# Sums and the gate-times-up product moved to GpSimd, and the runs of a seven-product scheme dealt to other gaps

## The chip, the cores and the metric

The kernel runs on one core of one Trainium2 chip. The metric is the device time of one execution in microseconds, as a median over runs. An execution is also profiled: the span is the time from the first to the last instruction of the program in that execution.

The engines are named as the profile names them: PE is TensorE's matrix multiply and PEld its weight load, DVE is VectorE, ACT is ScalarE, POOL is GpSimd, SP is SyncE, which here issues the transfers (DMA).

## The reference

One block of a network on 2048 tokens of 512 features: a layer norm, then sliding-window attention beside a SwiGLU feed-forward network, joined by a gate.

```python
def _A_ref(x, wqkv, wo):                      # H = 32 heads of Dh = 16, window W = 256
    qkv = (x @ wqkv).reshape(B, S, 3, H, Dh).transpose(2, 0, 3, 1, 4)
    q, k, v = qkv[0], qkv[1], qkv[2]
    scores = jnp.einsum("bhqd,bhkd->bhqk", q, k) * (Dh ** -0.5)
    mask = (idx[:, None] - idx[None, :] >= 0) & (idx[:, None] - idx[None, :] < W)
    p = _softmax(jnp.where(mask[None, None], scores, -1e9), axis=-1)
    o = jnp.einsum("bhqk,bhkd->bhqd", p, v)
    return o.transpose(0, 2, 1, 3).reshape(B, S, D) @ wo

def _B_ref(x, w1, w3, w2):                    # w1, w3: 512 x 1792; w2: 1792 x 512
    h = _silu(x @ w1) * (x @ w3)              # gate, up
    return h @ w2

xn = _layernorm(x)
return x + _A_ref(xn, A_wqkv, A_wo) * _silu(_B_ref(xn, B_w1, B_w3, B_w2))
```

Everything is fp32 at the interface.

## The kernel before

**Precision.** A large fp32 operand is held as two f16 halves, a high one and a low one (`hi` is the rounded value, `lo` the rest), in one tile of 128 x 1024. A product of two such operands is three f16 products, high by high, high by low and low by high, summed in one PSUM bank. Making such a pair is a copy to f16 and a subtraction: the helper `halves` (L341) does an operation in two parts of 256 columns, so many lines of the profile carry its line number, L344.

**Tiling.** The tokens are worked in four stages t = 0 to 3 of 512. The feed-forward network has 14 blocks f of 128 of its 1792 features. In stages 0 and 1 each block is computed directly (`gate_up`, L1002: gate and up for 512 tokens, 128x512 matmuls, line L1014). In stages 2 and 3, seven pairs j of blocks (2j, 2j + 1) are computed with seven products in place of eight (`quad`, L1147; a scheme of Strassen and Winograd over two blocks of features, two halves of the 512 features summed over, and two halves of the tokens). A product is 12 matmuls of 128x256 (L1168), half of the bank for gate and half for up. The seven products run in the order p1, p2, p6, p5, p7, p3, p4 and use two PSUM banks, a and b: p1, p6, p5 and p3 accumulate one on the other in a, p7 and p4 in b, and p2 has the other bank to itself. After p1, p6, p5 and p3 ScalarE copies bank a to a tile of `cpool` (`copied`, L1172, line L1175), so the next product that goes to bank a waits for that copy. After p2, p7 and p4 DVE adds the bank to an earlier copy (`added`, L1178, line L1180).

**What the scheme needs besides.** `weight_sums(j)` (L1049) loads the four raw weight blocks of a pair, scales them on ScalarE (L1066), forms four sums and differences of 128x256 for each of gate and up on DVE (L1070 to L1073), makes f16 pairs of them (copy on ScalarE L1079, subtraction on GpSimd), and eight steps later stores each to HBM as dSum (L1085), from where `load_quad` (L1135) fetches them. The seven calls lie in stages 1 and 2 (`QUAD_AT`). `token_sums(t)` (L1102) does the like for the tokens of stages 2 and 3: adds the two f16 halves (`both`, DVE, L344), four differences for each of two pairs on DVE (L1116 to L1119), and the f16 pairs (ScalarE L1124, GpSimd L344).

**Gate and up.** For a half block of 256 tokens, `activated` (L1185) takes the finished tile (gate in columns 0 to 255, up in 256 to 511). One step later ScalarE makes the tanh of gate (L1193); three steps later DVE makes (tanh + 1) x gate (L1197) and then multiplies by up (L1198). That is SiLU written with tanh; the constant factor sits in a scale. When both blocks are complete, each is made an f16 pair (`halved`: ScalarE L1250, GpSimd L344) for `down` (L1274, line L1286), the product with w2.

**Attention beside it.** The 32 units of attention (four stages, four groups of eight heads, two parts p) are cut into batches: "W" makes masked scores (TensorE L771, the mask added by DVE L778, the exponential by ScalarE L781), "M", "X" and "N" make the scores of a unit two ahead for its row maxima (TensorE L683, DVE L697), and the last batch of a unit multiplies probabilities by values (TensorE L799). Plans of five batches a unit are written out by hand (`PLAN`, L1484); the fourth is "WWX" and the fifth "NN" with the values.

**The order of the work.** TensorE executes in the order in which the code emits. The other engines' instructions are ordered by the framework's scheduler ahead of the run, with `urgent()` as a higher priority, and each engine then runs its list in order. `later(n, f)` puts f off by n steps, and a step is one batch or one piece of dense work. A unit's dense pieces (blocks of `gate_up`, the seven products, `down`, projections, values, totals) are dealt to the gaps behind its batches by `spread` (L1592): a piece's cost is its number of 512-column matmuls (6 for one of the seven products, 12.5 for the batch with the values), and pieces go behind a batch until their share of the whole is reached. Pieces marked `glued` stay with the next: the seven products come as four runs, p1 p2, then p6 with one other group behind it, then p5 p7, then p3 p4, with costs 12, 18 (with a group of 12), 12 and 12. `arranged` (L1518) sets other work between pairs j.

**Buffers.** 53 slots of 2 KB a partition serve nearly all tiles. `take` gives the slot that has been free longest; `give(tile, after=n)` marks it as to be used again n steps on. Where none else is free, a slot is taken before that, and its new writer waits for its last reader, which can be a store.

Of the kernel before, what the change touches and what calls it, by code (L numbers as in the profile page):

```python
# [15 lines left out]
ALU = mybir.AluOpType  # L16
# [34 lines left out]
TWO_ONES = struct.unpack("f", struct.pack("ee", ONE, ONE))[0]  # L51
VW = DH + 1
VB = 10
SLOTS = 53
ORDERED = {ENGINE.PE}
GROUPS = ((0, 4), (4, 8), (8, 11), (11, 14))
QUAD_FROM = 2
# [29 lines left out]
def tile_block(ctx: ExitStack, tc: tile.TileContext, x, wqkv, wo, w1, w3, w2, out):  # L87
    nc = tc.nc
# [3 lines left out]
    def pool(name, bufs, space=None):  # L92
        kw = {} if space is None else {"space": space}
        return ctx.enter_context(tc.tile_pool(name=name, bufs=bufs, **kw))
# [8 lines left out]
    ppool = pool("ppool", 5)  # L103
    opool = pool("opool", 2)
    fpool = pool("fpool", 2)
    cpool = pool("cpool", 5)
    psm = pool("psm", 1, PSUM)
    pss = pool("pss", 2, PSUM)
    pso = pool("pso", 1, PSUM)
# [2 lines left out]
    now = [0]  # L112
    free = [(0, i, f"slot{i}") for i in range(SLOTS)]
    held = {}
    given = [SLOTS]

    def take(dtype):
        free.sort()
        slot = free.pop(0)[2]
        made = fpool.tile([P, 512 if dtype == F32 else 1024], dtype, name=slot, tag=slot, bufs=1)  # L120
        held[id(made)] = slot, made
        return made

    def give(*tiles, after=0):

        for made in tiles:
            given[0] += 1
            free.append((now[0] + after, given[0], held.pop(id(made))[0]))
# [4 lines left out]
    def opening(pieces):  # L133

        for _, f in pieces[:-1]:
            f.opens = True
        return pieces
# [4 lines left out]
    def urgent():  # L142


        return tc.high_priority(offset=200) if started else nullcontext()
    made_so_far = [0]

    def later(n, f):
        made_so_far[0] += 1
        queue.append((now[0] + n, made_so_far[0], f))  # L150

    def step():
        now[0] += 1
        while True:
            due = min((q for q in queue if q[0] <= now[0]), default=None)
            if due is None:
                return
            queue.remove(due)
            due[2]()
# [77 lines left out]
    def behind_exp():  # L237

        return tc.issue_after(lasts["exp"].ins) if "exp" in lasts else nullcontext()

    def behind_load():

        return tc.issue_after(lasts["load"].ins) if "load" in lasts else nullcontext()
# [97 lines left out]
    def halves(op, out, a, b):  # L341

        for c in (slice(0, 256), slice(256, 512)):
            op(out[:, c], a[:, c], b[:, c])  # L344
# [657 lines left out]
    def gate_up(t, f):  # L1002
# [43 lines left out]
                later(1, rest)  # L1046
        return [q for k in range(2) for q in opening([(6, lambda k=k, half=half: part(k, half)) for half in range(2)])]

    def weight_sums(j):  # L1049

        cell = {}
        add, sub = nc.vector.tensor_add, nc.vector.tensor_sub
        l, r = slice(0, 256), slice(256, 512)

        def load(k):
            cell[k] = [take(F32) for _ in range(2)]
            w = (w1, w3)[k]
            for i, raw in enumerate(cell[k]):
                f = 2 * j + i
                lasts["load"] = nc.sync.dma_start(raw.rearrange("p (c f) -> p c f", f=P),  # L1060
                                                  w[:, f * P:(f + 1) * P].rearrange("(c p) f -> p c f", p=P))

        def scale(i, k):
            raw = cell[k][i]
            with behind_exp():
                nc.scalar.activation(raw, raw, AF.Copy, scale=inverses[:, j, k, i:i + 1])  # L1066

        def sums(k):
            a, b = cell[k]
            add(b[:, r], b[:, l], b[:, r])  # L1070
            sub(b[:, l], a[:, l], b[:, l])
            sub(a[:, l], b[:, r], a[:, l])
            sub(a[:, r], a[:, r], a[:, l])  # L1073

        def cut(i, k):
            raw = cell[k][i]
            made = take(F16)
            with behind_exp():
                nc.scalar.copy(made[:, 0:512], raw)  # L1079
            halves(nc.gpsimd.tensor_sub, made[:, 512:], raw, made[:, 0:512])  # L1080
            give(raw, after=20)

            def store():
                with behind_load():
                    nc.sync.dma_start(dSum[i, k, j], made)  # L1085
                give(made, after=10)
            later(8, store)

        def work():
            for k in range(2):  # L1090
                n = 8 * k
                later(n, lambda k=k: load(k))
                for i in range(2):
                    later(n + 10 + i, lambda i=i, k=k: scale(i, k))
                later(n + 12, lambda k=k: sums(k))
                for i in range(2):
                    later(n + 14 + 2 * i, lambda i=i, k=k: cut(i, k))
        return work
# [3 lines left out]
    def token_sums(t):  # L1102

        assert turned[t] == 4
        xh, xl = X[t]
        add, sub = nc.vector.tensor_add, nc.vector.tensor_sub
        l, r = slice(0, 256), slice(256, 512)
        whole = [take(F32) for _ in range(NC)]
        HALF[t] = [None] * NC

        def both(c):
            halves(add, whole[c], xh[:, c, :], xl[:, c, :])

        def sums(c):
            a, b = whole[c], whole[2 + c]
            sub(a[:, l], a[:, r], a[:, l])  # L1116
            sub(a[:, r], b[:, r], a[:, r])
            sub(b[:, r], b[:, r], a[:, l])
            sub(b[:, l], b[:, l], b[:, r])  # L1119

        def cut(c):
            HALF[t][c] = made = take(F16)
            with behind_exp():
                nc.scalar.copy(made[:, 0:512], whole[c])  # L1124
            halves(nc.gpsimd.tensor_sub, made[:, 512:], whole[c], made[:, 0:512])
            give(whole[c], after=20)
        n = 0
        for f, cs in ((both, (0, 2, 1, 3)), (sums, (0, 1)), (cut, (0, 2, 1, 3))):
            for c in cs:
                later(n, lambda f=f, c=c: f(c))  # L1130
                n += 2
# [15 lines left out]
    def quad(t, j):  # L1147
# [37 lines left out]
        def activated(f, half, made):  # L1185

            if "h" not in cell.setdefault(f, {}):
                cell[f]["h"] = take(F32)
            h = cell[f]["h"][:, 256 * half:256 * half + 256]

            def tangent():
                with urgent():
                    nc.scalar.activation(h, made[:, 0:256], AF.Tanh, scale=sg_apart[:, f:f + 1])  # L1193

            def gated():
                with urgent():
                    nc.vector.scalar_tensor_tensor(h, h, 1.0, made[:, 0:256], op0=ALU.add, op1=ALU.mult)  # L1197
                    nc.vector.tensor_mul(h, h, made[:, 256:512])  # L1198
            if final:
                tangent()  # L1200
                gated()
                return
            later(1, tangent)
            later(3, gated)
# [50 lines left out]
        ahead = (t, j + 1) if j < FB // 2 - 1 else (t + 1, 0)  # L1255
        pieces = []
# [9 lines left out]
            opening(run)  # L1266
        for i in (0, 3, 5):
            pieces[i][1].glued = True
        return pieces

    ACC = {}
# [121 lines left out]
    def feed_forward():  # L1393
# [5 lines left out]
        def sums_of(t, at):  # L1399

            made = []
            if (t, at) in sums_at:
                made.append((0, weight_sums(sums_at[t, at])))
            for to, where in HALVES_AT.items():
                if where == (t, at):
                    made.append((0, lambda to=to: token_sums(to)))
            return made
# [61 lines left out]
    whole = sum(c for c, _ in ffn)  # L1469
# [112 lines left out]
    def in_runs(dense):  # L1582

        runs = []
        for piece in dense:
            if runs and getattr(runs[-1][-1][1], "glued", False):
                runs[-1].append(piece)
            else:
                runs.append([piece])
        return runs  # L1590

    def spread(made, dense):  # L1592

        whole = sum(c for c, _ in dense) + sum(c for c, _ in made)
        dense = in_runs(dense)
        at = 0
        for k, (cost, batch) in enumerate(made):
            batch()
            step()
            at += cost  # L1600
            while dense:
                c = sum(c for c, _ in dense[0])
                if c and at + c / 2 > whole * (k + 1) / len(made):
                    break
                at += c
                run(dense.pop(0))
        run([piece for r in dense for piece in r])

    def run(dense):
        for c, piece in dense:  # L1610
            piece()
            if c:
                step()
# [102 lines left out]
    ahead = [[] for _ in units]  # L1716
# [16 lines left out]
    for n, u in enumerate(units):  # L1733
# [25 lines left out]
        dense = [piece for _, k, i in both for piece in lists[k][i]]  # L1759
# [3 lines left out]
        k = n // 2 + 2  # L1763
# [35 lines left out]
```

## Time and profile before

| | |
|---|---|
| median of 3 runs | 850.73 us (846.98 to 852.57) |
| profiled execution, its own time | 850.31 us |
| its span | 848.5 us |
| mean granted TensorE clock | 0.994 |
| busy: PE, DVE, ACT, POOL | 794.3, 688.9, 450.5, 277.3 us |
| first and last start of the seven products' matmuls (L1168) | 429.0 and 818.5 us |

A busy row of the page gives us, share of the span and number of instructions. A row of the waits names the engine and line that stood idle, what it waited for, and then the total in us, the number of waits and the longest. A row of groups gives line, engine, operation, tiles, shapes and count, then busy time in us and the mean of one in ns, then the engine's idle time ahead of them and what ended it. A row of the timeline gives start and duration in us, the instruction, and in brackets the idle time before it with what ended that.

### The profile page before, as it was taken

What the parts mean: (1) busy time and instruction counts of PE and PEld (TensorE: products, weight loads), DVE (VectorE), ACT (ScalarE), POOL (GpSimd) and SP (SyncE); (2) the same over time, 40 slices, a digit from 0 to 9 for tenths busy, and PEclk for the clock granted to TensorE, in tenths of its full rate; (3) what the DMA queues carried; (4) which work ended last, traced back from release to release, by engine and by line L of the source; (5) the groups of instructions that cost most, each with busy time, mean ns of one, the idle gap of its engine ahead of it and who ended that gap; (6) DMA issues with size and microseconds to landing.
All of it is one profiled execution on the core that took longest, in us unless ns stands there. A gap on an engine that the chain in (4) does not pass through costs nothing. (4 is left out here: it accounts for less than half of the span.)

```text
span 848.5 us, 24657 instructions
## 1 busy us (share of the span) xinstructions
PE 794.3 (94%) x9433; PEld 431.6 (51%) x9433; DVE 688.9 (81%) x2181; ACT 450.5 (53%) x692; POOL 277.3 (33%) x545
## 2 busy tenths in 40 slices
PE   9999999999999999899988987999999988997998
PEld 4444444444454444444455654545565565655664
DVE  8878898887988788988999897679787877875655
ACT  6897797553254555336465464434454544544531
POOL 2364747441242343412545141030232111131310
PEclk9999999999999999999999999999999999999999
DMA  9877556446555667274755756445465554252411
GB/s 289 270 239 239 176 177 206 158 148 200 148 181 152 204 184 219 80 259 135 250 186 138 246 171 199 146 125 193 146 169 181 149 170 143 60 169 83 121 46 51
DMA packets 130119, 144.33 MB, mean 170 GB/s; under 512 B 19472, under 2 KB 87888, under 8 KB 130000
## 3 DMA queue, kind: packets, MB, share of 16 engines
q1 hardware_dynamic: 129712, 142.23, 54.2%
q8 instruction: 74, 1.21, 0.6%
q10 hardware_dynamic: 288, 0.52, 0.2%
q14 instruction: 45, 0.37, 0.2%
HBM read 100.40 MB, written 37.49 MB: 163 GB/s over the span
## 5 line engine op out<-in xcount | busy, mean ns | idle before, releaser
L781 ACT ACTIVATE pt<-s,es 128x1024 f32<-128x1024 f32 x152 | 167.5, 1112 | 205.1 <-DVE s L778 198.9
L344 POOL TENSOR_TENSOR slot<-slot,slot 128x256 f16<-128x256 f32 (+1 forms) x208 | 140.8, 702 | 410.9 <-ACT slot L1250 153.0
L1286 PE MATMUL m<-slot,slot 128*128 128x512 f16 x672 | 156.2, 382 | 6.3 <-ACT copy L1175 4.3
L697 DVE CUSTOM_DVE_ANT_0 junk<-s,MW 128x320 bf16<-128x320 f32 x276 | 133.4, 483 | 9.3 <-PE s L683 2.4
L778 DVE TENSOR_TENSOR s<-s,MK 128x256 f32<-128x256 f32 (+2 forms) x280 | 116.9, 432 | 28.4 <-PE s L771 25.7
L1014 PE MATMUL m<-XH,slot 128*128 128x512 f16 x448 | 133.7, 380 | 1.3 <-DVE slot L1342 0.8
L1168 PEld LDWEIGHTS <-slot 128*128 128x128 f16 x1176 | 111.8, 98 | 38.7 <-issue 22.8
L1286 PEld LDWEIGHTS <-slot 128*128 128x128 f16 x672 | 62.3, 98 | 83.8 <-issue 14.7
L1014 PEld LDWEIGHTS <-slot 128*128 128x128 f16 x672 | 62.4, 98 | 78.9 <-issue 7.8
L697 DVE CUSTOM_DVE_ANT_0 junk<-po,MW 128x320 bf16<-128x320 f32 x172 | 83.4, 485 | 3.7
L1168 PE MATMUL m<-slot,slot 128*128 128x256 f16 x672 | 80.6, 273 | 5.7 <-ACT copy L1175 3.4
L1014 PE MATMUL m<-XL,slot 128*128 128x512 f16 x224 | 84.9, 379 | 0.0
L613 PE MATMUL m<-XH,slot 128*128 128x512 f16 x240 | 72.6, 388 | 7.4 <-DVE slot L1342 5.5
L799 PE MATMUL po<-pt,V 64*32 64x320 f32 (+4 forms) x2880 | 77.2, 342 | 1.4 <-DVE XL L535 1.1
L1168 PE MATMUL m<-XH,slot 128*128 128x256 f16 x336 | 57.0, 273 | 9.3 <-ACT copy L1175 5.3
L613 PEld LDWEIGHTS <-slot 128*128 128x128 f16 x392 | 37.3, 99 | 51.4 <-issue 12.5
L771 PE MATMUL s<-qa,KA 50*64 50x320 f16 (+3 forms) x1472 | 58.8, 260 | 4.1 <-DVE M L697 3.2
L799 PEld LDWEIGHTS po<-pt,V 64*32 64x32 f32 x2880 | 51.1, 106 | 22.4 <-issue 1.7
L360 POOL TENSOR_TENSOR slot<-slot,slot 128x128 f16<-128x128 f32 x112 | 46.7, 452 | 47.8 <-ACT slot L357 47.7
L771 PEld LDWEIGHTS <-KA 50*64 50x64 f16 x1472 | 30.5, 106 | 53.7 <-issue 31.2
L683 PE MATMUL s<-KA,qa 48*64 48x320 f16 (+3 forms) x824 | 45.6, 295 | 9.3 <-DVE M L697 3.9
L1180 DVE SCALAR_TENSOR_TENSOR copy<-m,copy 128x512 f32<-128x512 f32 x42 | 28.9, 687 | 29.7 <-PE m L1168 16.6
(190 smaller groups left out, 1212.1 us busy)
## 6 DMA issues: line engine op xcount, KB each, us to landing
slot<-dW SPq DMA_DIRECT2D x112, 256.0 KB
slot<-in_B_w_dram SPq DMA_DIRECT2D x70, 256.0 KB
slot<-dSum SPq DMA_DIRECT2D x56, 256.0 KB
dW<-slot SPq DMA_DIRECT2D x42, 256.0 KB
slot<-in_A_x_dram SPq DMA_DIRECT2D x30, 256.0 KB
dSum<-slot SPq DMA_DIRECT2D x28, 256.0 KB
KA<-dK SPq DMA_DIRECT2D x24, 288.0 KB
slot<-dWQ SPq DMA_DIRECT2D x24, 256.0 KB
```

The lines of the kernel that those rows point to most:

```text
L344: op(out[:, c], a[:, c], b[:, c])
L360: nc.gpsimd.tensor_sub(lo[:, c // 2, at], raw[:, c * P:(c + 1) * P], hi[:, c // 2, at])
L613: nc.tensor.matmul(cell["pp"][:, cols[n]], w[:, (a * NC + c) * P:(a * NC + c + 1) * P], b[:, c, cols[n]], start=n == 0 and (c, i) == parts ...
L683: nc.tensor.matmul(s[c:c + w, r, :n], qa[rows, 2 * p + a, ii * P + c:ii * P + c + w], ka[rows, 2 * p + a, e - n:e], start=True, stop=True)
L697: lasts["maximum"] = nc.vector.tensor_tensor_reduce(out=junk[:, :n], in0=s[:, r, :n], in1=mask, scale=1.0, scalar=NEG, op0=ALU.add, op1=AL ...
L771: nc.tensor.matmul(s[64 * h:64 * h + 64, r, o:o + 64 * n], ka[rows, 2 * p + a, 64 * (m + 4):64 * (m + 5)], qa[rows, 2 * p + a, 64 * (m + k ...
L778: nc.vector.tensor_add(v, v, MK[:, kind, of:of + n, :].unsqueeze(1).to_broadcast([P, 2 * len(which), n, 64]))
L781: lasts["exp"] = nc.scalar.activation(pt, s, AF.Exp, scale=es)
L799: nc.tensor.matmul(cell["po"][32 * i:32 * i + 32, h, 64 * (m + k):64 * (m + k + n)], V[64 * h:64 * h + 64, (4 * t + m // 2) % VB, hd * VW: ...
L1014: nc.tensor.matmul(cell[k], w[:, at:at + P], b[:, c, :], start=c == 0 and i == 0, stop=c == NC - 1 and i == 2)
L1168: nc.tensor.matmul(ps[:, 256 * k:256 * k + 256], w(k, a, c), x(b, c), start=first and k == 0 and c == 0 and n == 0, stop=k == 1 and c == 1 ...
L1286: nc.tensor.matmul(ps, hh[:, a * TW + b * P:a * TW + (b + 1) * P], w[:, c * D:(c + 1) * D], start=f == f0 and i == 0, stop=f == f1 - 1 and ...
```

## The change

Four things change.

- In `weight_sums` and `token_sums` all adds and subtractions go from DVE to GpSimd, and the f16 copies go from ScalarE to GpSimd: the new `in_halves` copies 256 columns and subtracts 256 columns, twice.
- In `activated`, GpSimd multiplies gate by up in place (ahead of the tanh in the same step), and DVE makes (tanh + 1) x (gate x up) in one instruction; DVE's multiplication goes.
- Units in which some of the seven products are dealt no longer use `spread`'s rule but the new `by_gaps`. It searches all ways to cut the list of runs into consecutive lots, one for each gap, for the smallest sum of ((cost of the lot - aim) / 6) squared, plus 16 for two neighbouring runs in one lot that are both short and 3 where one of the two is. Short are the runs that hold products of the scheme; p3 gets a mark so that its run counts. The aim is the unit's whole cost over the number of gaps, less the cost of the gap's own batch.
- 53 slots become 51, and the copy buffers (`cpool`) 5 become 7.

```diff
--- before.py
+++ after.py
@@ -51,7 +51,7 @@
 TWO_ONES = struct.unpack("f", struct.pack("ee", ONE, ONE))[0]
 VW = DH + 1
 VB = 10
-SLOTS = 53
+SLOTS = 51
 ORDERED = {ENGINE.PE}
 GROUPS = ((0, 4), (4, 8), (8, 11), (11, 14))
 QUAD_FROM = 2
@@ -103,7 +103,7 @@
     ppool = pool("ppool", 5)
     opool = pool("opool", 2)
     fpool = pool("fpool", 2)
-    cpool = pool("cpool", 5)
+    cpool = pool("cpool", 7)
     psm = pool("psm", 1, PSUM)
     pss = pool("pss", 2, PSUM)
     pso = pool("pso", 1, PSUM)
@@ -1046,10 +1046,16 @@
                 later(1, rest)
         return [q for k in range(2) for q in opening([(6, lambda k=k, half=half: part(k, half)) for half in range(2)])]
 
+    def in_halves(made, raw):
+
+        for c in (0, 256):
+            nc.gpsimd.tensor_copy(made[:, c:c + 256], raw[:, c:c + 256])
+            nc.gpsimd.tensor_sub(made[:, 512 + c:768 + c], raw[:, c:c + 256], made[:, c:c + 256])
+
     def weight_sums(j):
 
         cell = {}
-        add, sub = nc.vector.tensor_add, nc.vector.tensor_sub
+        add, sub = nc.gpsimd.tensor_add, nc.gpsimd.tensor_sub
         l, r = slice(0, 256), slice(256, 512)
 
         def load(k):
@@ -1075,9 +1081,7 @@
         def cut(i, k):
             raw = cell[k][i]
             made = take(F16)
-            with behind_exp():
-                nc.scalar.copy(made[:, 0:512], raw)
-            halves(nc.gpsimd.tensor_sub, made[:, 512:], raw, made[:, 0:512])
+            in_halves(made, raw)
             give(raw, after=20)
 
             def store():
@@ -1103,7 +1107,7 @@
 
         assert turned[t] == 4
         xh, xl = X[t]
-        add, sub = nc.vector.tensor_add, nc.vector.tensor_sub
+        add, sub = nc.gpsimd.tensor_add, nc.gpsimd.tensor_sub
         l, r = slice(0, 256), slice(256, 512)
         whole = [take(F32) for _ in range(NC)]
         HALF[t] = [None] * NC
@@ -1120,9 +1124,7 @@
 
         def cut(c):
             HALF[t][c] = made = take(F16)
-            with behind_exp():
-                nc.scalar.copy(made[:, 0:512], whole[c])
-            halves(nc.gpsimd.tensor_sub, made[:, 512:], whole[c], made[:, 0:512])
+            in_halves(made, whole[c])
             give(whole[c], after=20)
         n = 0
         for f, cs in ((both, (0, 2, 1, 3)), (sums, (0, 1)), (cut, (0, 2, 1, 3))):
@@ -1190,12 +1192,12 @@
 
             def tangent():
                 with urgent():
+                    nc.gpsimd.tensor_mul(made[:, 256:512], made[:, 0:256], made[:, 256:512])
                     nc.scalar.activation(h, made[:, 0:256], AF.Tanh, scale=sg_apart[:, f:f + 1])
 
             def gated():
                 with urgent():
-                    nc.vector.scalar_tensor_tensor(h, h, 1.0, made[:, 0:256], op0=ALU.add, op1=ALU.mult)
-                    nc.vector.tensor_mul(h, h, made[:, 256:512])
+                    nc.vector.scalar_tensor_tensor(h, h, 1.0, made[:, 256:512], op0=ALU.add, op1=ALU.mult)
             if final:
                 tangent()
                 gated()
@@ -1266,6 +1268,7 @@
             opening(run)
         for i in (0, 3, 5):
             pieces[i][1].glued = True
+        pieces[5][1].after_quad = True
         return pieces
 
     ACC = {}
@@ -1589,10 +1592,47 @@
                 runs.append([piece])
         return runs
 
+    def by_gaps(made, dense, whole):
+
+        runs = []
+        ahead = []
+        for one in dense:
+            ahead = ahead + one
+            if sum(c for c, _ in one):
+                runs.append(ahead)
+                ahead = []
+        costs = [sum(c for c, _ in r) for r in runs]
+        short = [any(hasattr(f, "quad") or hasattr(f, "after_quad") for _, f in r) for r in runs]
+        n = len(made)
+        best = {(0, 0): (0, ())}
+        for g in range(n):
+            aim = max(whole / n - made[g][0], 0)
+            for i in range(len(runs) + 1):
+                if (g, i) not in best:
+                    continue
+                for j in range(i, len(runs) + 1):
+                    bad = ((sum(costs[i:j]) - aim) / 6)**2
+                    for k in range(i, j - 1):
+                        bad += 16 if short[k] and short[k + 1] else 3 if short[k] or short[k + 1] else 0
+                    bad += best[g, i][0]
+                    if (g + 1, j) not in best or best[g + 1, j][0] > bad:
+                        best[g + 1, j] = bad, best[g, i][1] + (j,)
+        ends = best[n, len(runs)][1]
+        at = 0
+        for (_, batch), end in zip(made, ends):
+            batch()
+            step()
+            run([piece for r in runs[at:end] for piece in r])
+            at = end
+        run(ahead)
+
     def spread(made, dense):
 
         whole = sum(c for c, _ in dense) + sum(c for c, _ in made)
         dense = in_runs(dense)
+        if any(hasattr(f, "quad") or hasattr(f, "after_quad") for run_ in dense for _, f in run_):
+            by_gaps(made, dense, whole)
+            return
         at = 0
         for k, (cost, batch) in enumerate(made):
             batch()
```

## The prediction

> **What bounds the kernel now.** I read the head of the page first, then the busy time by stage, then what TensorE waited for in the stage that holds the seven products (425 us to the end).
>
> ```profile
> span 848.5 us, 24657 instructions
> PE 794.3 (94%) x9433; PEld 431.6 (51%) x9433; DVE 688.9 (81%) x2181; ACT 450.5 (53%) x692; POOL 277.3 (33%) x545
> ```
>
> ```profile
> 250.00:440.00 190.00, 184.31 (x2181) 88.50 (x2180) 163.95 (x501) 94.64 (x128) 65.11 (x108) 0.99 0.60 183
> 440.00:530.00 90.00, 74.44 (x1155) 47.94 (x1153) 80.46 (x237) 48.99 (x72) 31.70 (x48) 0.99 0.63 192
> 530.00:848.50 318.50, 292.82 (x3612) 179.09 (x3610) 234.92 (x680) 140.12 (x199) 65.55 (x103) 0.99 0.43 130
> ```
>
> The columns are the window, its length, then PE, PEld, DVE, ACT and POOL busy, the granted clock, DMA share and GB/s. TensorE sets the time: it is idle for 54 us of 848.5, so no more than that can be won without taking work off it, and the change takes none off. From 250 to 440 us it is idle 3% of the time. From 440 to 530 it is idle 15.6 us of 90 and DVE is 89% busy; after that it is idle 25.7 us of 318.5 and DVE is 74% busy. The gain is to be looked for in what TensorE waits for there:
>
> ```profile
> PE m L1168 <- ACT copy L1175: 8.7, 8, 1.7
> PE m L613 <- DVE slot L1342: 5.5, 2, 5.3
> PE m L1286 <- ACT copy L1175: 4.3, 4, 1.2
> PE s L683 <- DVE M L697: 3.9, 4, 1.3
> PE m L1168 <- DVE slot L1310: 2.8, 4, 1.3
> PE s L683 <- ACT pt L781: 2.4, 4, 0.7
> PE s L723 <- DVE NM L717: 1.8, 1, 1.8
> PE m L1168 <- DVE slot L634: 1.7, 2, 1.0
> PE m L1168 <- DMA slot<-dW: 1.6, 1, 1.6
> PE m L613 <- DVE slot L634: 1.4, 1, 1.4
> ```
>
> There are three kinds: 13.0 us in 12 waits for the ScalarE copy of a product's bank (8.7 + 4.3); 11.6 us for DVE being late with ordinary work (3.9 + 2.8 + 1.8 + 1.7 + 1.4); and one wait of 5.3 us of a kind of its own.
>
> **The change part by part.** The sum is made against the profiled execution: 850.3 us, of which 848.5 are the span and 1.8 lie around it; the median of the three runs is 850.7.
>
> *What leaves DVE and ScalarE.* The rows are line, engine, shape, count, then busy us and mean ns.
>
> ```profile
> L1198 DVE TENSOR_TENSOR slot<-slot,copy 128x256 f32<-128x256 f32 x56 | 27.0, 482 | 0.7
> L1073 DVE TENSOR_TENSOR slot<-slot 128x256 f32<-128x256 f32 x14 | 8.0, 572 | 0.1
> L1072 DVE TENSOR_TENSOR slot<-slot,slot 128x256 f32<-128x256 f32 x14 | 5.8, 417 | 0.2
> L344 DVE TENSOR_TENSOR slot<-XH,XL 128x256 f32<-128x256 f16 x16 | 7.3, 481 | 3.9 <-POOL slot L344 3.0 <-DMA out_dram<-slot 0.7 <-PE m L1014 0.2
> L1116 DVE TENSOR_TENSOR slot<-slot 128x256 f32<-128x256 f32 x4 | 1.7, 416 | 0.0
> L1079 ACT CAST slot<-slot 128x512 f16<-128x512 f32 x28 | 16.8, 618 | 5.7 <-DVE slot L1073 4.8 <-DMA dQ<-slot 0.8 <-DVE slot L1071 0.2
> L1124 ACT CAST slot<-slot 128x512 f16<-128x512 f32 x8 | 4.8, 615 | 0.0
> ```
>
> DVE loses 27.0 us of products (56), about 27 of weight sums (four lines of 14, between 5.8 and 8.0 each), and 14.1 of token sums (7.3, and four lines of 4 like L1116): 68 us, from 689 to 621. ScalarE loses 16.8 + 4.8 = 21.6 us of 450; it has idle time, so I book that at nothing.
>
> *What GpSimd gets.*
>
> ```profile
> L344 POOL TENSOR_TENSOR on<-on,rb 128x256 f32<-128x256 f32 x32 | 22.9, 737 | 40.6 <-DMA rb<-de 31.4 <-DMA dr<-os 8.5 <-issue 0.6
> L869 POOL CAST slot<-on 128x256 f16<-128x256 f32 x30 | 11.6, 413 | 2.8 <-PE m L1286 2.8
> ```
>
> Fp32 operations of that shape: 56 weight sums, 56 products, 16 token differences, 128 x 0.737 = 94 us. 16 adds from f16 to fp32: not in the trace; the two rows bound them by 0.41 and 0.74, and with two inputs they are nearest the upper one: 0.70, 11 us. 72 copies of 128x256 at 0.413: 30 us. GpSimd goes from 277 to 412 us, 49% of the span. It is nowhere full. Five blocks of weight sums (9.2 us each) and a set of token sums (15) put 61 us on top of 65 from 250 to 440; two blocks and 16 products put 30 on top of 31.7 of 90 from 440 to 530; 40 products and a set of token sums 44 on top of 65.6 behind that. So the stores to dSum, whose issue on SP waits for GpSimd as it does now, cost nothing in my sum, since they are issued eight steps behind the cut; if GpSimd falls behind by more than that, the weight loads and the maxima's transfers queued on SP behind them come late.
>
> *A: the wait at 340 us.* The token sums of stage 2 begin here on DVE:
>
> ```profile
> 339.16 1.68 DVE L344 TENSOR_TENSOR slot<-XH,XL 128x256 f32<-128x256 f16 x2 [1.54 <-POOL slot L344]
> 342.38 0.42 PE L771 MATMUL s<-qa,KA 50*64 50x320 f16 x12 [2.02 <-DVE M L697]
> 300.00:350.00 50.00, 46.96 (x555) 21.64 (x561) 43.18 (x127) 26.57 (x38) 19.61 (x30) 0.97 0.57 172
> 500.00:550.00 50.00, 40.07 (x541) 22.76 (x526) 39.05 (x125) 22.73 (x33) 12.76 (x20) 0.93 0.54 168
> ```
>
> DVE stood 1.54 us for a buffer that GpSimd still held, the masks and maxima behind it came late, TensorE stood 2.02 us, and the granted clock of that stage is 0.97, another 0.03 x 50 = 1.5 us. On GpSimd, which held the buffer, the adds stall nobody. **-3.5 us.**
>
> *B: DVE late.* In 440 to 530 us about 17 of DVE's 80.5 us go (20 weight sums, the products of four quads); behind 530 some 26 of 235 (ten quads, one set of token sums). The moved operations also disturb what stays, since they are the ones that stretch beside GpSimd:
>
> ```profile
> L1198 DVE TENSOR_TENSOR slot<-slot,copy x56: 360/424/933, 435.7 to 820.9; 128x256 f32<-128x256 f32 x56
> L778 DVE TENSOR_TENSOR s<-s,MK x280: 285/423/700, 58.8 to 811.8; 128x256 f32<-128x256 f32 x128, 128x512 f32<-128x512 f32 x12
> ```
>
> (minimum/median/maximum ns; L778's maximum is that of its double-length form). Bounds 0 and -11.6; with a fifth of DVE's load gone where it is fullest and a tenth elsewhere, I take half: **-5.8 us.**
>
> *C: the dealing.* Before, a stage with 18 of other work, runs of 12, 18, 12 and 12 of the seven, and a last batch of 12.5 gives its gaps 18, 12, 18, 24 and 0: the fifth and seventh product stand beside the third and fourth. By the new function (aim 16.9, in the last gap 4.4; 16 for two short runs side by side) the deal is 18, 12, 18, 12, 12. What this is about:
>
> ```profile
> 689.98 2.12 ACT L781 ACTIVATE pt<-s,es 128x1024 f32<-128x1024 f32 x2 [1.82 <-DVE s L778]
> 692.63 0.38 PE L1168 MATMUL m<-XH,slot 128*128 128x256 f16 x2 [1.68 <-ACT copy L1175]
> 441.19 0.33 PE L683 MATMUL s<-KA,qa 48*32 48x320 f16 x8 [0.73 <-ACT pt L781]
> 442.20 0.33 PE L683 MATMUL s<-KA,qa 48*32 48x320 f16 x8 [0.67 <-ACT pt L781]
> 470.98 0.33 PE L683 MATMUL s<-KA,qa 48*32 48x320 f16 x8 [0.67 <-ACT pt L781]
> ```
>
> The third product waited 1.68 us because its bank's copy stood behind two exponentials. With a batch between, that wait goes. But the first two units of stage 2 are dealt 12 and 12 at that place already, and there the narrow scores of the next batch wait for those same exponentials: of the 2.4 us in the list above, 1.40 fall in one unit and the rest in the other. So most of the wait moves rather than goes. Bounds -13.0 (nothing moves) and +1 (all 12 come back, the mean of 1.04 us against 1.08, and a unit that had none gets one); I take **-4 us.**
>
> *D: two slots fewer.* Of 53 slots two become copy buffers. The 5.3 us wait is one for a slot:
>
> ```profile
> 522.62 1.47 SPq L1085 DMA_DIRECT2D dSum<-slot  x1
> 526.48 0.63 ACT L1332 ACTIVATE slot<-slot 128x512 f32<-128x512 f32 x1 [1.30 <-DMA dSum<-slot]
> 528.68 0.59 PE L613 MATMUL m<-XH,slot 128*128 128x512 f16 x1 [5.32 <-DVE slot L1342]
> ```
>
> A tanh was given the slot of a dSum store still under way, and with it the clock fell (0.93 in that stage, 3.5 us): 8.8 us in all. It may go, stay, or come twice; **0**, bounds -8.8 and +17.6.
>
> *E: DVE waits for GpSimd.* The gated step (L1197) now waits for tanh and for GpSimd's product.
>
> ```profile
> L1193 ACT ACTIVATE slot<-copy,sga 128x256 f32<-128x256 f32 x56 | 28.0, 508 | 39.7 <-DVE copy L1180 39.3
> POOL on L344 <- DMA rb<-de: 14.0, 2, 9.6
> ```
>
> Alone, the product ends 0.737 - 0.508 = 0.23 us after tanh, 56 x 0.23 = 13 us of DVE waits at most; behind two subtractions in GpSimd's order, 1.3 us more; behind a multiply that waits for its transfer, up to 9.6. What queues behind it on DVE are masks and maxima, for which exponentials and TensorE wait. The step is due three steps behind its product, and DVE will be idle about a third of the time behind 530 us; that hides most, and without it the 13 us count in full: **+2 us**, bounds 0 and +31 (13 us, and a quarter of the 56 behind two subtractions, 18).
>
> Sum: 850.3 - 3.5 - 5.8 - 4 + 0 + 2 = **839.0 us.**
>
> The Trainium skill has a rule against this change: in "Perfetto Trace Analysis", Optimizing Scalar/DVE Operations, it warns that offloading between GpSimd and DVE might not help since they share a read port, and "SBUF — State Buffer", Who interferes with whom, names a DVE operation with two SBUF inputs as one that blocks against GpSimd's reads. By that rule L1197, which stays, would suffer; the trace agrees as far as L1198's 933 ns against L778's unstretched form with one PSUM input. What it would make of the time is the port case below.
>
> **The rivals.**
> *Better:* the moved waits do not return (C -9) and the slot wait goes (D -8.8): 825. For it: DVE brings masks, and so exponentials, earlier. Against: 51 slots.
> *The wait only changes place* (C 0, B half): 850.3 - 3.5 - 2.9 + 2 = 846. For it: the L683 rows above. The new dealing then does not do what it says, and where pairs stood apart already it changes nothing.
> *Slots:* one or two more waits like that at 523 us: 848 to 857, say 851. Against: each needs a store caught in flight.
> *Port:* GpSimd is busy half the time instead of a third, every second L1197 doubles as L1198's maximum does (28 x 0.5 = 14 us of DVE), B is nil and 4 us more reach TensorE: 850.3 - 3.5 - 4 + 2 + 4 = 849.
> *Slower, GpSimd's queue:* in-order GpSimd holds the product behind subtractions and transfers, DVE stands before L1197 and all 31 us reach TensorE: 839 - 2 + 31 = 868. It decides from about 13 us, a quarter of a microsecond per product. For it: the 9.6 us wait. Against: GpSimd idle two thirds of the time behind 530 us (110 busy of 318.5).
>
> **How the numbers follow.** Forecast 0.43, better 0.17, place 0.14, slots 0.10, port 0.06, GpSimd's queue 0.10. One per cent, about what a measurement of this kernel can tell from no change, is 8.5 us: under 842.2 is faster, over 859.2 slower. Of the forecast (839, give or take 5) 0.06 lies within. Faster 0.37 + 0.17 = 0.54; within 0.06 + 0.14 + 0.10 + 0.06 = 0.36; slower 0.10. Range 825 to 857, from the better case to two more slot waits.
>
> **What would show it.** Right: DVE near 621 us, GpSimd near 412; no DVE wait on GpSimd and no TensorE wait near 340 us; "m <- ACT copy" down from 13.0 us, and "L683 <- ACT pt" up from 2.4. Wrong: DVE's gated step waiting for GpSimd for more than 13 us in total, TensorE idle over 54 us, more waits on slots whose stores are in flight, or the 13.0 us all gone with nothing in their place.

## The result, and the profile after

The changed kernel takes 845.75 us (median of 18 runs, 843.14 to 848.01) against 851.61 us of the kernel before on the same chips; the ratio is 0.9929 (95% interval 0.9916 to 0.9942). It is 0.7% faster, about 6 us, where 11.3 us were forecast. The profiled execution took 845.49 us.

The head of the page and the slices of the granted clock, after:

```profile
span 843.7 us, 24735 instructions
PE 797.4 (95%) x9433; PEld 435.4 (52%) x9433; DVE 641.9 (76%) x2037; ACT 432.6 (51%) x656; POOL 400.2 (47%) x761
PEclk9999999999999999999998997999999999999999
```

DVE lost 47 us and not 68, GpSimd gained 123. TensorE's idle time fell from 54.2 us to 46.3 (843.7 - 797.4), but its busy time rose by 3.1 for the same instructions, and the granted clock was lower: 0.986 of full speed on average instead of 0.994, which is 11.8 us of the span instead of 5.1. The stages, in the columns shown for the kernel before:

```profile
250.00:440.00 190.00, 186.29 (x2308) 91.71 (x2295) 147.43 (x460) 87.92 (x113) 123.92 (x218) 1.00 0.61 189
440.00:530.00 90.00, 74.18 (x1017) 45.93 (x1015) 63.95 (x185) 39.08 (x56) 51.46 (x87) 0.89 0.58 175
530.00:843.70 313.70, 293.81 (x3614) 181.50 (x3612) 220.69 (x627) 138.69 (x196) 109.22 (x171) 0.99 0.44 133
```

From 440 to 530 us DVE's load fell from 80.5 to 64.0 us, as worked out, and yet TensorE stood still as long as before (15.8 us of 90, before 15.6), with the clock at 0.89. What TensorE waited for over the whole span, and below it the one new line of DVE's waits:

```profile
PE s L771 <- ACT pt L781: 6.9, 2, 6.5
PE s L683 <- ACT pt L781: 5.4, 12, 0.7
PE m L1289 <- DVE slot L1313: 4.5, 3, 3.9
PE po L683 <- DVE M L697: 4.0, 2, 3.2
PE m L1289 <- DVE copy L1182: 3.3, 2, 1.7
```

```profile
DVE slot L1200 <- POOL copy L1195: 40.7, 27, 5.1
```

The waits for ScalarE's copies (13.0 us) are gone altogether. In their place stand a few long waits, 6.5, 3.9 and 3.2 us, and DVE's gated step (now L1200) waits 40.7 us for GpSimd's product (L1195). The timeline shows that these are one thing. Around 500 us, GpSimd's instructions and those that stand behind them on the other engines:

```profile
499.95 1.41 POOL L344 TENSOR_TENSOR on<-on,rb 128x256 f32<-128x256 f32 x2
501.30 0.74 POOL L1052 CAST slot<-slot 128x256 f16<-128x256 f32 x2
502.00 1.30 POOL L1053 TENSOR_TENSOR slot<-slot,slot 128x256 f16<-128x256 f32 x2
503.36 0.74 POOL L869 CAST slot<-on 128x256 f16<-128x256 f32 x2
504.06 0.72 POOL L1195 TENSOR_TENSOR copy<-copy 128x256 f32<-128x256 f32 x1
504.74 1.48 POOL L344 TENSOR_TENSOR slot<-on,slot 128x256 f16<-128x256 f32 x2
504.82 0.87 DVE L1200 SCALAR_TENSOR_TENSOR slot<-slot,copy 128x256 f32<-128x256 f32 x1 [5.08 <-POOL copy L1195]
...
506.21 0.68 DVE L778 TENSOR_TENSOR s<-s,MK 128x512 f32<-128x512 f32 x1
...
506.93 1.11 ACT L781 ACTIVATE pt<-s,es 128x1024 f32<-128x1024 f32 x1
...
508.10 0.64 PE L771 MATMUL s<-qa,KA 50*64 50x320 f16 x8 [6.48 <-ACT pt L781]
```

GpSimd has no gap here: it works off multiplies of attention and the f16 pairs of a weight sum (L1052, L1053), the product comes behind them, DVE stands 5.08 us with the next mask queued behind the gated step, the exponential waits for the mask, and TensorE stands 6.48 us for the exponential. The same with weight sums at 447 us and with token sums at 588 us:

```profile
447.84 0.93 DVE L1200 SCALAR_TENSOR_TENSOR slot<-slot,copy 128x256 f32<-128x256 f32 x1 [2.25 <-POOL copy L1195]
...
450.02 2.29 PE L1289 MATMUL m<-slot,slot 128*128 128x512 f16 x5 [3.88 <-DVE slot L1313]
```

```profile
588.52 0.93 DVE L1200 SCALAR_TENSOR_TENSOR slot<-slot,copy 128x256 f32<-128x256 f32 x1 [2.90 <-POOL copy L1195]
...
590.45 0.33 PE L683 MATMUL po<-KA,qa 48*64 48x320 f16 x4 [3.23 <-DVE M L697]
```

So the theory was that the dealing and the sums gain, and that the product takes it back, above all where it meets the sums in GpSimd's queue. The rivals were that the long waits come from the shorter lots or from two slots fewer, that the product costs the same wherever it stands, and that it is GpSimd's load, not DVE's wait, that costs.

### The profile page after: what moved, and what is told of

Its sections match the earlier page's. It is cut to its first block, busy times and chain, and to the rows that moved or that the text cites. A ratio compares the mean times of both kernels' runs of the same rounds, so it can differ in the third digit from the quotient of the medians.

```text
span 843.7 us, 24735 instructions
## 1 busy us (share of the span) xinstructions
PE 797.4 (95%) x9433; PEld 435.4 (52%) x9433; DVE 641.9 (76%) x2037; ACT 432.6 (51%) x656; POOL 400.2 (47%) x761
## 4 chain that ended last, share of the span: by engine, by line
PE 60%; DVE 15%; POOL 7%; ACT 6%; issue 6%; DMA 4%; SPq 2%; DVEq 0%; POOLq 0%; ACTq 0%
PE m L1014 12%; PE m L1289 12%; PE m L1170 8%; PE m L613 8%; PE po L799 6%; DVE junk L697 4%; PE s L771 4%; PE m L577 3%; PE m L1341 3%; DVE s L778 2%; PE s L683 2%; POOL slot L344 2%; ACT pt L781 1%; SPq L854 1%; POOL copy L1195 1%
## 5 line engine op out<-in xcount | busy, mean ns | idle before, releaser
L1289 PE MATMUL m<-slot,slot 128*128 128x512 f16 x672 | 160.3, 390 | 8.9 <-DVE slot L1313 4.5
L778 DVE TENSOR_TENSOR s<-s,MK 128x256 f32<-128x256 f32 (+2 forms) x280 | 117.8, 433 | 43.5 <-PE s L771 40.7
L344 POOL TENSOR_TENSOR slot<-slot,slot 128x256 f16<-128x256 f32 (+1 forms) x136 | 89.8, 680 | 121.1 <-ACT slot L1043 55.9
L1195 POOL TENSOR_TENSOR copy<-copy 128x256 f32<-128x256 f32 x56 | 40.5, 726 | 120.7 <-DVE copy L1182 98.7
L1170 PE MATMUL m<-slot,slot 128*128 128x256 f16 x672 | 82.5, 276 | 0.2
L771 PE MATMUL s<-qa,KA 50*64 50x320 f16 (+3 forms) x1472 | 58.6, 260 | 8.6 <-ACT pt L781 6.9
L1200 DVE SCALAR_TENSOR_TENSOR slot<-slot,copy 128x256 f32<-128x256 f32 x56 | 33.4, 597 | 40.7 <-POOL copy L1195 40.7
L799 PEld LDWEIGHTS po<-pt,V 64*32 64x32 f32 x2880 | 53.1, 106 | 20.5 <-PE s L683 2.0
L771 PEld LDWEIGHTS <-KA 50*64 50x64 f16 x1472 | 30.3, 106 | 57.0 <-issue 41.1
```

What stands on the lines that cost most here:

```text
L771: nc.tensor.matmul(s[64 * h:64 * h + 64, r, o:o + 64 * n], ka[rows, 2 * p + a, 64 * (m + 4):64 * (m + 5)], qa[rows, 2 * p + a, 64 * (m + k ...
L778: nc.vector.tensor_add(v, v, MK[:, kind, of:of + n, :].unsqueeze(1).to_broadcast([P, 2 * len(which), n, 64]))
L799: nc.tensor.matmul(cell["po"][32 * i:32 * i + 32, h, 64 * (m + k):64 * (m + k + n)], V[64 * h:64 * h + 64, (4 * t + m // 2) % VB, hd * VW: ...
L1170: nc.tensor.matmul(ps[:, 256 * k:256 * k + 256], w(k, a, c), x(b, c), start=first and k == 0 and c == 0 and n == 0, stop=k == 1 and c == 1 ...
L1195: nc.gpsimd.tensor_mul(made[:, 256:512], made[:, 0:256], made[:, 256:512])
L1289: nc.tensor.matmul(ps, hh[:, a * TW + b * P:a * TW + (b + 1) * P], w[:, c * D:(c + 1) * D], start=f == f0 and i == 0, stop=f == f1 - 1 and ...
```

## The experiments

Each run's ratio is to the kernel before on the same chip.

| kernel | median, us | ratio (95% interval) |
|---|---|---|
| dealing alone | 828.84 | 0.9742 (0.9722 to 0.9762) |
| sums alone | 836.88 | 0.9831 (0.9814 to 0.9849) |
| product alone | 861.64 | 1.0125 (1.0104 to 1.0146) |
| dealing and sums | 823.54 | 0.9677 (0.9660 to 0.9695) |
| dealing and product | 836.38 | 0.9823 (0.9804 to 0.9842) |
| all three (the change) | 845.75 | 0.9929 (0.9916 to 0.9942) |

**The change without the product.** `activated` as before:

```diff
-                    nc.gpsimd.tensor_mul(made[:, 256:512], made[:, 0:256], made[:, 256:512])
                     nc.scalar.activation(h, made[:, 0:256], AF.Tanh, scale=sg_apart[:, f:f + 1])
...
-                    nc.vector.scalar_tensor_tensor(h, h, 1.0, made[:, 256:512], op0=ALU.add, op1=ALU.mult)
+                    nc.vector.scalar_tensor_tensor(h, h, 1.0, made[:, 0:256], op0=ALU.add, op1=ALU.mult)
+                    nc.vector.tensor_mul(h, h, made[:, 256:512])
```

> The changed kernel with the product of gate and up back on DVE (dealing, sums on GpSimd, 51 slots stay). Theory Q (the product stands in GpSimd's queue behind the sums, DVE stands before its gated step, TensorE stands 3.9 + 6.5 + 3.2 us and the clock falls for another 6.8 us): those waits go and DVE gets 27 us back, so about 830 us, with no TensorE wait over 2.5 us between 440 and 600 us. Rival S (those waits come from the shorter lots and two slots fewer, the product only stood where something else would have stood): 844 to 848 us, with waits of 3 us and more still there.

823.54 us, 0.9677: more than 20 us under the changed kernel. The waits at 446, 501 and 587 us are gone; one of 5.6 us is left, for a slot (below). The rival that held the lots or the slots responsible falls, since both are still in this kernel.

**The dealing alone.** `weight_sums`, `token_sums` and `activated` as before; `by_gaps`, 51 slots and 7 copy buffers of the change.

> The kernel before with the dealing, 51 slots and 7 copy buffers alone; sums and product stay on DVE, copies on ScalarE. Theory Q: the 13.0 us of TensorE waits for ScalarE's copies go and about 3 us come back as waits for exponentials: about 842 us. Rival (the wait only changes place, and two slots fewer cost): 850 us or more.

828.84 us: 22 us, two and a half times what even the theory expected. What TensorE waited for at exponentials, and the stage from 530 us:

```profile
PE s L683 <- ACT pt L781: 6.9, 14, 0.7
PE s L771 <- ACT pt L781: 2.2, 3, 1.2
```

```profile
530.00:820.00 290.00, 282.75 (x3561) 175.85 (x3554) 228.29 (x665) 138.55 (x198) 66.58 (x102) 1.00 0.46 138
```

No wait for ScalarE's copies is left (13.0 us before), and some of it did come back, in the narrow scores as read from the first units of stage 2: over the span L683's waits for exponentials rose from 3.3 to 6.9 us and L771's from 0.4 to 2.2. But the balance is far better than forecast: TensorE is busy 97.5% of 530 to 820 us, before 92.4% of the same stretch (268.0 us of 290).

The 22 us can be told apart by adding up all of TensorE's waits in the two traces. Waits for copies fell by 13.0 us and 5.4 came back at exponentials; waits for DVE fell from 29.9 to 20.8; waits for transfers and TensorE's own fell by 2.7; and the clock, 0.997 instead of 0.994, is worth another 2.6. Not all of this is the dealing. Of the 9 us at DVE, 3.6 are the wait behind the tanh's slot (5.3 before, 1.7 here) and 2.0 the wait at 340 us. The latter is gone in this kernel although the sums still begin on DVE and no product is dealt so early: the first one starts at 425.9 us, 3 us earlier than before. That leaves the slots as its likely cause, not tried by themselves. That more even lots made DVE late less often can account for the remaining 3.5 us at most, and is argued. The rival that the two more copy buffers, and not the dealing, ended the waits for copies falls with the kernel of 53 slots and 5 copy buffers below, which has the new dealing and no such wait; and the sums alone, with the old dealing, still have 11.8 us of them.

**The sums alone** (old dealing, 53 slots, product on DVE):

```diff
-        add, sub = nc.vector.tensor_add, nc.vector.tensor_sub
+        add, sub = nc.gpsimd.tensor_add, nc.gpsimd.tensor_sub
...
-            with behind_exp():
-                nc.scalar.copy(made[:, 0:512], raw)
-            halves(nc.gpsimd.tensor_sub, made[:, 512:], raw, made[:, 0:512])
+            in_halves(made, raw)
```

> The kernel before with weight and token sums and their f16 copies on GpSimd alone; old dealing, 53 slots, product on DVE. Theory Q: the wait at 340 us and its clock go (3.5 us) and part of DVE's lateness from 440 to 530 us: about 844 us. Rival (GpSimd's reads slow what DVE keeps as much as DVE is relieved): 850 to 852 us.

836.88 us, 0.9831, a larger gain than the 844 expected. No TensorE wait at 340 us is left (nor is it in the dealing alone), the first product starts 7.3 us earlier than before, and DVE is less full from 440 to 530 us (72.4 us of 90, before 80.5):

```profile
440.00:530.00 90.00, 74.70 (x1052) 46.80 (x1050) 72.37 (x215) 41.02 (x58) 46.35 (x75) 0.96 0.60 184
```

On top of the dealing the same sums gain 0.0065 of 851 us, 5.5 us, instead of 14: the two relieve the same waits in part, the one at 340 us among them.

**The product alone** (old dealing, sums on DVE; the `activated` of the change).

> The kernel before with the product of gate and up on GpSimd alone; old dealing, sums on DVE. Theory Q (the product costs where it meets the sums in GpSimd's queue): without the sums there DVE waits 13 to 20 us for GpSimd instead of 40.7, in small pieces, and the time is 848 to 853 us. Rival (the product on GpSimd costs by itself, wherever it stands): DVE waits 35 us or more and the time is 856 us or more.

```profile
DVE slot L1198 <- POOL copy L1193: 28.2, 29, 2.6
```

861.64 us, 1.0125: the product costs 11 us by itself. DVE's wait lies between the two expectations, 28.2 us in 29 small pieces, the time beyond that of the rival. So the collision is not the whole of it.

**Dealing and product** (the change with the sums back on DVE and the f16 copies on ScalarE).

> The changed kernel with the sums back on DVE and the f16 copies on ScalarE (dealing and product of the change stay). Collision theory: little of the product's price is left without the sums in GpSimd's queue, 830 to 835 us. Even theory (11 us as in the old dealing, or more): 838 to 842 us.

```profile
DVE slot L1204 <- POOL copy L1199: 23.0, 22, 4.0
```

836.38 us. Beside the dealing alone the product costs 0.9823 - 0.9742, 0.0081 or 7 us; beside dealing and sums it costs 0.9929 - 0.9677, 0.0252 or 21 us. The 836.38 us fall between the two expectations. The other 14 us are the meeting of product and sums.

**The product on GpSimd in stage 3 alone,** where no sums are made, the rest as changed:

```diff
+                    if t == 3:
                         nc.gpsimd.tensor_mul(made[:, 256:512], made[:, 0:256], made[:, 256:512])
```

with the gated step of the change where t is 3 and that of before elsewhere.

> The changed kernel with the product on GpSimd in stage 3 alone (28 of 56), on DVE in stage 2, where the sums share GpSimd's queue. Collision theory (the product costs where it meets the sums): no TensorE wait of 3 us between 440 and 600 us but the one for a slot, 824 to 829 us. Even theory (each product costs the same): half of the 22.2 us, so 833 to 836 us.

829.50 us, 0.9742 (0.9726 to 0.9758): the 28 products of stage 3 cost 0.0065, 5.5 us, and the 28 of stage 2 the other 0.0187, 16 us. The theory's 824 to 829 is missed by half a microsecond, the even price by three and a half; the waits of 3 us and more are gone but for the one for a slot (5.7 us). DVE waits 17.0 us here, all in stage 3:

```profile
DVE slot L1202 <- POOL copy L1196: 17.0, 14, 3.8
```

So DVE's wait is not the price by itself. In the changed kernel stage 3 has about as much of it as here, 17 us, with two waits of 3.8 us behind attention's multiplies and no sum near, and TensorE stands 1.7 and 1.6 us behind those two. The 17 us cost 5.5; the other 23 us, in stage 2, cost 16.

**The product made and not read.** Dealing and sums with the gated step on DVE, and GpSimd multiplies besides, into a tile that nobody reads:

```diff
+                    nc.gpsimd.tensor_mul(unread, made[:, 0:256], made[:, 256:512])
                     nc.scalar.activation(h, made[:, 0:256], AF.Tanh, scale=sg_apart[:, f:f + 1])
```

> The 823.5 us kernel (dealing and sums on GpSimd, gated step and its product on DVE) with GpSimd doing the same 56 products besides, into a tile that nobody reads. The result is the reference's. Wait theory (the product costs because DVE stands in order before its gated step until GpSimd gives the product): 823 to 827 us, GpSimd busy 40 us more. Load theory (GpSimd's 40 us more of reads and its fuller queue cost by themselves: DVE's operations with two SBUF inputs stretch, the f16 pairs come late): 835 to 845 us.

```profile
PE 791.3 (96%) x9433; PEld 433.3 (52%) x9433; DVE 660.8 (80%) x2093; ACT 431.4 (52%) x656; POOL 406.9 (49%) x761
```

827.42 us, 0.9717 (0.9698 to 0.9735), 0.4 us over the wait theory's 823 to 827 and far from the load theory's 835: GpSimd does 42 us more (364.9 without) and the kernel loses 0.0040, 3.4 us, of the 21; the wait for a slot is 1.5 us longer in this trace (7.1 us, without the product 5.6). The rest of the price is DVE's wait, by elimination.

**The gated step two steps later.** `later(5, gated)` for `later(3, gated)` in the changed kernel.

> The changed kernel with the gated step put off by five steps instead of three. Wait theory, with the scheduler's order as its cause (DVE's gated step stands too early in DVE's list): DVE's 40.7 us of waits for GpSimd fall under 15 us and the time is 826 to 834 us. If two steps change nothing in the lists (the scheduler puts the step where its own model says the product is done): 843 to 848 us and waits of 35 us or more.

```profile
DVE slot L1200 <- POOL copy L1195: 39.8, 26, 5.1
```

845.94 us, 0.9936 (0.9919 to 0.9953), and 39.8 us of waits: nothing. Put in order of time, the instructions of each engine come in the same order by line and tile in both traces, DVE's 2037 and GpSimd's 761 among them. The edit changed no list, so this experiment does not tell what a later place in DVE's list would bring.

**Slots.** In the 823.5 us kernel one wait of before was still there:

```profile
514.87 0.63 ACT L1335 ACTIVATE slot<-slot 128x512 f32<-128x512 f32 x1 [6.43 <-DMA dSum<-slot]
517.53 1.01 PE L613 MATMUL m<-XH,slot 128*128 128x512 f16 x2 [5.61 <-DVE slot L1345]
```

The tanh of a total is given the slot of a dSum store under way, as in the kernel before. Three kernels ask what it hangs on: 53 slots and 5 copy buffers; 51 and 7 with

```diff
-                give(made, after=10)
+                give(made, after=30)
```

in `weight_sums`; and both.

> The 823.5 us kernel (dealing and sums of the change, product on DVE) with the buffers of before: 53 slots and 5 copy buffers. Term D by itself. If the two slots are what the wait for a store in flight hangs on, it shortens from 5.6 us or goes, and the clock does not fall: 815 to 820 us. If the copy buffers are needed by the new dealing, waits for the copies come back: 826 us or more. If neither: 822 to 825 us.

> The 823.5 us kernel with the slots of the dSum stores marked as free 30 steps on instead of 10, so that the tanh at 512 us and the residual's load are given other slots. Theory (that wait is one for a store in flight, 5.6 us, and the clock falls behind it for 3.4 us more): the wait goes and the time is 813 to 817 us. Rival (with 51 slots some other slot in use is given instead): 821 us or more, with a wait of several us elsewhere.

> Both: 53 slots, 5 copy buffers, and the slots of the dSum stores marked as free 30 steps on. Theory: as the better of the two or up to 2 us below it, 812 to 816 us. Rival: 821 us or more.

820.45 us, 0.9642 (0.9624 to 0.9661); 815.81 us, 0.9593 (0.9573 to 0.9613); 818.13 us, 0.9617 (0.9597 to 0.9637). With 53 slots the wait is still 4.7 us, and the time lies between the expectations. With the later mark it is gone, and so is every fall of the clock in the profiled execution (0.997 to 1.000 over the four executions):

```profile
PE m L613 <- DVE slot L1345: 4.7, 1, 4.7
```

```profile
core 0: 813.7 us, clock 1.000
```

(the first of 53 slots, the second of the later mark alone). The wait, with the clock behind it, was worth 0.0084, 7 us, and hung on which slot was given: two slots more shortened it by 0.9 us. Both edits together miss their 812 to 816 us and are not better than the later mark alone; why is open. The 815.81 us kernel is the fastest found, 4.1% under the one before.

## Why the prediction was wrong

*What bounds the kernel* was right: TensorE with waits behind 440 us, of the three kinds named.

*The loads* were right for the most part. GpSimd came to 400 us (412 said); the rows taken from elsewhere held: the product takes 726 ns (737 from another fp32 row). DVE came to 642 and not 621. Of these 21 us 8 are the gated step's, which now meets GpSimd: 597 ns on average where it was 450 (56 x 0.147), up to 940. The rest is a mistake of reading: recorded durations on DVE overlap their neighbours' (in the kernel before a mask of 0.43 us starts at 430.53 and the next instruction at 430.87), so that taking an instruction away frees less than its duration. Added up over the span, DVE's durations fell by 58.4 us (818.7 to 760.3), its busy time by 47.0.

```profile
L1200 DVE SCALAR_TENSOR_TENSOR slot<-slot,copy 128x256 f32<-128x256 f32 x56 | 33.4, 597 | 40.7 <-POOL copy L1195 40.7
L1200 DVE SCALAR_TENSOR_TENSOR slot<-slot,copy x56: 414/425/940, 428.9 to 816.2; 128x256 f32<-128x256 f32 x56
```

*A and B* (-3.5 and -5.8, together -9.3) lie between what the sums gained alone, 14 us, and on top of the dealing, 5.5. A gave the sums a wait that also goes without moving them.

*C* (-4 us) was mis-sized by a factor of five. The dealing, with its slots and buffers, gained 22 us alone. One step that failed is "so most of the wait moves rather than goes": the waits for copies went from 13.0 to nothing, and those for exponentials rose by 5.4, so that 7.6 us went for good. The prediction read two units right and priced all others by them. The larger part lay outside the term: 9.1 us less of waiting for DVE, 2.7 at transfers and TensorE's own, and 2.6 of the clock.

*D* (0) was rightly open: the wait is worth 7 us, against 8.8 worked out. In the changed kernel it is hardly seen, 1.3 us at 528, perhaps because the longer waits ahead of it give the store its time; that is not shown, and in the dealing alone, which has no such waits, it is 1.7 us. Two slots fewer have no clear price: with the early mark 53 slots and 5 buffers were 3 us faster, with the later mark 2 us slower.

*E* (+2 us) is the term that decided. It measured 21 us. The step that failed: "the step is due three steps behind its product, and DVE will be idle about a third of the time behind 530 us; that hides most". DVE's idle time hides far less than that, because DVE works in order: at 504 us it stands before the gated step while the mask that TensorE needs is queued behind it. And the two parts of the change were priced apart, the sums by GpSimd's busy share and the product by two subtractions ahead of it, while from 440 to 530 us they stand in one queue: at 504 us the product had at least eight instructions ahead of it without a gap. The prediction's own sum had GpSimd busy 62 of the 90 us there (30 on top of 31.7; 51.5 measured), but weighed the queue by its idle time behind 530 us. The rival "GpSimd's queue" had the mechanism, with 31 us for DVE's waits where 40.7 were measured, and was given 0.10; that all of them reach TensorE was too much, since the price, with DVE's relief in it, was 21. It did not make the kernel slower because dealing and sums gained 27.5 us together.

*The port* case is the smaller part. The gated step does stretch: in the changed kernel it takes 868 ns on average where GpSimd works beside it for over 30% of its time (22 of 56) and 421 ns elsewhere, while the masks of 128x256, with one input from PSUM, take 411 and 406 ns. But the unread product puts the load and the port together at 3.4 us. That is an estimate of their part in the change and no bound: the two DVE steps stretch by 4.5 us there (30.3 + 29.2 us against 27.5 + 27.5 without it), the one step of the changed kernel by 5.9 (597 ns against 491). The Trainium skill's rule in "Perfetto Trace Analysis", Optimizing Scalar/DVE Operations, that offloading between DVE and GpSimd might not help because they share a read port, came true for the product, though mostly by the wait and not by the port, and did not for the sums, which gained 1.7% by themselves. The Trainium skill's "SBUF — State Buffer", Who interferes with whom, says that a DVE instruction with two SBUF inputs contends with a GpSimd instruction that reads SBUF; the trace agrees with L1200's 940 ns.

So the forecast of 839 us was the sum of a gain half as large as measured (13.3 us against 27.5) and a loss ten times too small (2 against 21). That the measured time lies within the stated range of 825 to 857 us is luck: the two errors cancel in part.

## What to carry to other kernels

Work moved to a slower engine pays where nobody waits for its result soon, and costs where a full, in-order engine stands for it: price it by the queue that it meets, with what the same change adds to that queue, and ask what stands behind the waiting instruction. Try the parts of a change by themselves, since here one part hid four fifths of the gain of the other two. Where a long wait names a store that has nothing to do with the work, look at which buffer was given before looking for more buffers.

## What the runs showed of the hardware

The clock costs beside the long waits. The kernel with the later mark has no TensorE wait over 1.5 us behind 440 us and a granted clock of 1.000 in its profile; the changed kernel, with waits of 3.9, 6.5 and 3.2 us, has 0.986, which is 11.8 us of its span, beside 13.6 us of those waits. In windows of 2 us its clock reads 0.50 from 448 to 454, from 506 to 516 and from 592 to 594 us, late in those waits or behind them. It also reads 0.50 from 466 to 468 us, behind a wait of 1.4 us, and 1.00 behind waits of 1.7 and 1.6 us at 699 and 748 us. So the length of a wait alone does not tell here whether the clock falls.
